# Scatters of different batches declared independent of each other, with a small memset ahead of each

## The chip, the cores and the metric

The kernel runs on one core of a Trainium2 chip. The metric is the device time of one execution in microseconds (us), the median of several runs. The core has five engines that run their own instruction streams side by side: TensorE (PE, matrix products), VectorE (DVE), ScalarE (ACT), GpSimd (POOL) and the sync engine (SP), which here issues plain transfers. They are tied together by semaphores. A transfer between the chip's main memory and the engines' memory is done by 16 DMA engines; an instruction only issues it, and a semaphore tells when it has landed.

## The reference

An attention with a sliding window feeds a layer in which only some tokens pass through an MLP (mixture of depths). There are 8 batches of 576 tokens, 8 heads of 64.

```python
# attention, window 128, with a linear bias by head
scores = scale * np.matmul(q, k.transpose(0, 1, 3, 2))
scores = np.where(mask, scores + bias[None], -1000000000.0)
attn = softmax(scores)                       # cut: written out in the reference
x = (attn @ v).transpose(0, 2, 1, 3).reshape(B, S, H * D)    # 8 x 576 x 512

# mixture of depths
scores = np.einsum('bsd,d->bs', x, w_gate)
out = x.copy()
for b in range(B):
    top_idx = np.argpartition(-scores[b], capacity)[:capacity]   # 128 of 576 tokens
    xe = x[b, top_idx]
    h = np.maximum(xe @ w1, 0.0)
    ye = h @ w2
    g = 1.0 / (1.0 + np.exp(-scores[b, top_idx]))
    out[b, top_idx] = x[b, top_idx] + g[:, None] * ye
```

For each batch, all 576 rows of `x` go to the output, and 128 of them get something added.

## The kernel before

The kernel is scheduled by hand: a list of words, `ORDER`, gives the order in which steps are issued, and each engine runs its own steps in that order. `b` is the batch. The output is built in two moves: `store` writes all rows of `x` of a batch (issued by the sync engine), and `scatter` adds the 128 changed rows with an indirect DMA that takes row numbers from `tok` (issued by GpSimd). The framework places waits between instructions that touch the same tensor. All stores and scatters touch the tensor `out`, so without further word each would wait for those before it; `declare_no_dep` tells the framework that a pair needs no wait.

```python
def store(b, part):
    if part == 0:
        i = SP.dma_start(out=out[b, 0:512, :]..., in_=x32[b][:, 0:4, :])      # cut
    else:
        i = SP.dma_start(out=out[b, 512:, :], in_=x32[b][:64, 4, :])
    stores.append((b, i))
    for o, j in scatters:
        tc.declare_no_dep(_ins(i), _ins(j), reason="other rows")

def w2(b):                                   # last product of a batch (TensorE), L654
    t = mm_t[b, "y"] = mx()
    for f in range(NFC):
        PE.matmul(out=t, lhsT=hs[b][:, f, :], rhs=w2_bf[:, f, :],
                  start=(f == 0), stop=(f == NFC - 1))

def w2_copy(b, eng):                         # its result times the gate: the rows to add, L661
    fin[b] = mod.tile([128, HD], fp32, name="fin", bufs=NFIN)        # NFIN = 4 buffers
    t = mm_t.pop((b, "y"))
    if eng is ACT:
        ACT.activation(out=fin[b], in_=t, func=AF.Identity, scale=gsel[b][:, 2:3])
    ...                                      # cut

def scatter(b):                              # L667
    i = POOL.indirect_dma_start(
        out=out.flatten_outer_dims(),
        out_offset=bass.IndirectOffsetOnAxis(ap=tok[b][:, :1], axis=0),
        in_=fin[b], in_offset=None, compute_op=OP.add)

    for o, j in stores:
        if o != b:
            tc.declare_no_dep(_ins(i), _ins(j), reason="other rows")
    scatters.append((b, i))
```

Before the change a scatter is thus free of the stores of other batches, but it waits for the stores of its own batch, for its rows, and for the scatter issued before it.

In `ORDER`, `Fb` is the scatter of batch b, `zb/A` is `w2_copy` on ScalarE, `Zb` is `w2`, `Wb0` and `Wb1` are the two halves of the first MLP product and `wb0`, `wb1` the copies of their results, `Ob` is the one-hot matrix `oh` that selects the tokens, `Db` the gather with it. The tail of the list (all of it is at the end of the whole kernel):

```text
J7 r6 H7
B7 h7/D O6/D Z5 b7/A E7 e6 M73 M70 D6 z5/A M72 F5 K6 M71 v6/A
k6 R7 e7 W61 F4 M74 r7 O7/D W60 w61/A D7 w60/A Z6 v7/D W71
z6/A F6 W70 w71/D K7 w70/A k7 Z7 z7/A F7
```

So the scatters are issued in the order of batches 0, 1, 2, 3, 5, 4, 6, 7, and the last instruction of the whole list is the scatter of batch 7.

Of the kernel before, what the change touches and what calls it, by code (L numbers as in the profile page):

```python
# [10 lines left out]
fp32 = mybir.dt.float32  # L11
# [15 lines left out]
def kernel(  # L27
# [12 lines left out]
    PE, DVE, ACT, POOL, SP = (nc.tensor, nc.vector, nc.scalar, nc.gpsimd,  # L40
                              nc.sync)
# [19 lines left out]
    const = ctx.enter_context(tc.tile_pool(name="const", bufs=1))  # L61
# [183 lines left out]
    def c_slope(c):  # L245
        def eo_(x):
            return x.rearrange("p (y s) -> p s y", s=2)
# [2 lines left out]
            in0=eo_(tmp[:, 1, :]), scalar=float(2.0 ** (2 - c)),  # L250
            in1=eo_(tmp[:, 0, :]), op0=OP.mult, op1=OP.add)

    ones_bf = const.tile([128, 128], bf16)
    neg1 = const.tile([128, 1], bf16)
    one_f = const.tile([128, 1], fp32)
# [214 lines left out]
    stores, scatters = [], []  # L470

    def _ins(i):
        return getattr(i, "inst", None) or getattr(i, "ins", i)
# [190 lines left out]
            DVE.tensor_scalar_mul(out=fin[b], in0=t, scalar1=gsel[b][:, 2:3])  # L664

    def scatter(b):
        i = POOL.indirect_dma_start(  # L667
            out=out.flatten_outer_dims(),
            out_offset=bass.IndirectOffsetOnAxis(ap=tok[b][:, :1], axis=0),
            in_=fin[b], in_offset=None, compute_op=OP.add)  # L670

        for o, j in stores:
            if o != b:
                tc.declare_no_dep(_ins(i), _ins(j), reason="other rows")
        scatters.append((b, i))

    wst = {}
# [215 lines left out]
```

## Time and profile before

| | before |
|---|---|
| time, median of 3 runs | 170.21 us (170.15 to 170.29) |
| span of the profiled execution | 168.3 us |
| TensorE busy | 129.8 us (77%) |
| VectorE busy | 127.8 us (76%) |
| ScalarE busy | 123.9 us (74%) |
| GpSimd busy | 105.4 us (63%) |
| scatters: GpSimd busy with them | 13.3 us, 8 of them, 1667 ns each in the mean |
| scatters: GpSimd idle ahead of them | 21.9 us |
| scatters: from start to landing, least / median / most | 4.6 / 4.7 / 7.0 us |

How to read it: the time is measured from outside, the span is that of one execution taken by the hardware profiler, a little shorter. A busy share is an average over the span; an engine that is busy three quarters of it can still set the end, and one that is rarely busy can be the one that all wait for at the end. For a scatter the profile shows two things: the time in which GpSimd writes the transfer's descriptors (`DMA_INDIRECT` on POOL, line 667), and the landing, known from its semaphore. In brackets behind an instruction stands the idle time of its engine just before it and what ended it; "issue" there means that the profile shows nothing that it waited for at that moment, often because another instruction of the queue held the wait.

Rows of the engines over the span are given in 40 equal slices, with a digit for the busy share in tenths.

### The profile page before, as it was taken

How to read it: one execution, taken by the hardware profiler on the slowest of the kernel's cores; microseconds unless marked ns; L12 is line 12 of the kernel's file. 1: busy time of each engine (PE TensorE's matmuls, PEld its weight loads, DVE VectorE, ACT ScalarE, POOL GpSimd, SP SyncE). 2: the span in 40 equal slices, each digit the busy share in tenths (PEclk: the TensorE clock that was granted, in tenths of full speed). 3: DMA queues.
4: the chain of work that ended last, by engine and by line, in shares of the span. 5: the costliest groups of instructions: out<-in, count | busy, mean ns of one | idle time of the engine just before them, and what ended most of it. 6: DMA issues, size and time to landing. Idle time of an engine off the chain costs nothing. (4 is left out here: it accounts for less than half of the span.)

```text
span 168.3 us, 5059 instructions
## 1 busy us (share of the span) xinstructions
PE 129.8 (77%) x2029; PEld 103.9 (62%) x2029; DVE 127.8 (76%) x378; ACT 123.9 (74%) x148; POOL 105.4 (63%) x168
## 2 busy tenths in 40 slices
PE   0165987778759869996599998999999999998200
PEld 0152766556649747995386987878588867686000
DVE  6885377989897899899868999898997898942000
ACT  1667679999888999969968997998987854423100
POOL 3835766659845996788299995785697813213330
PEclk9999999999978999999879999999999999999965
DMA  4999999999999999999999999999009349344224
GB/s 154 279 282 378 372 331 275 353 405 284 395 333 410 358 357 418 382 333 372 325 308 406 381 350 292 360 372 254 11 0 292 60 62 294 55 62 66 23 39 62
DMA packets 35216, 44.38 MB, mean 264 GB/s; under 512 B 1652, under 2 KB 24440, under 8 KB 35192
## 3 DMA queue, kind: packets, MB, share of 16 engines
q1 hardware_dynamic: 33464, 41.69, 75.2%
q0 software_dynamic: 1152, 2.10, 9.4%
q8 instruction: 16, 0.26, 0.6%
q10 hardware_dynamic: 576, 0.26, 0.6%
q14 instruction: 8, 0.07, 0.1%
HBM read 32.51 MB, written 11.53 MB: 262 GB/s over the span
## 5 line engine op out<-in xcount | busy, mean ns | idle before, releaser
L439 ACT ACTIVATE P<-sc 128x2048 bf16<-128x2048 f32 x32 | 60.1, 1877 | 9.6 <-PE sc L430 7.3
L307 POOL TENSOR_SCALAR_AFFINE_SELECT v_bf<-v_st 64x512 bf16<-64x512 f32 x42 | 30.7, 734 | 12.1 <-DMA v_st<-in_v_dram 10.3
L506 DVE CUSTOM_DVE_ANT_0 x_bf<-x,wg_bc 128x512 bf16<-128x512 f32 x35 | 28.1, 837 | 0.1
L466 DVE TENSOR_TENSOR x<-at,rc 128x640 f32<-128x640 f32 x32 | 26.4, 824 | 1.3 <-DVE rc L464 0.2
L667 POOL DMA_INDIRECT out_dram<-fin,tok x8 | 13.3, 1667 | 21.9 <-issue 11.8
L414 PE MATMUL sc<-mQ,mK 64*128 64x512 bf16 x128 | 20.8, 404 | 7.8 <-ACT P L439 7.8
L430 PEld LDWEIGHTS <-kT 64*128 64x128 bf16 x384 | 20.9, 114 | 8.7 <-issue 2.1
L457 PE MATMUL at<-v_bf,P 128*128 128x66 bf16 x320 | 24.3, 198 | 1.8 <-ACT P L439 0.9
L307 POOL TENSOR_SCALAR_AFFINE_SELECT q_bf<-q_st 128x576 bf16<-128x576 f32 x24 | 18.2, 779 | 9.1 <-DMA q_st<-in_q_dram 8.1
L457 PEld LDWEIGHTS <-P 128*128 128x128 bf16 x320 | 21.3, 101 | 2.3 <-ACT P L439 1.1
L454 PE MATMUL at<-v_bf,P 128*128 128x66 bf16 x256 | 22.1, 198 | 0.0
L430 PE MATMUL sc<-qT,kT 64*128 64x256 bf16 (+2 forms) x384 | 21.6, 248 | 0.0
L331 PE MATMUL mx<-ident_bf,q_bf 128*128 128x128 bf16 x144 | 13.4, 233 | 10.3 <-DVE q_bf L313 6.9
L547 DVE TENSOR_SCALAR_CACHE_REDUCE cmp<-row,sc_all 128x64 bf16<-128x64 f32 (+4 forms) x40 | 20.2, 537 | 0.8 <-ACT row L337 0.8
L454 PEld LDWEIGHTS <-P 128*128 128x128 bf16 x256 | 18.8, 101 | 0.7 <-issue 0.5
L307 POOL TENSOR_SCALAR_AFFINE_SELECT k_bf<-k_st 128x512 bf16<-128x512 f32 (+1 forms) x26 | 17.9, 704 | 0.5
L331 PEld LDWEIGHTS <-q_bf 128*128 128x128 bf16 x144 | 9.9, 104 | 11.9 <-DVE q_bf L313 6.9
L637 PE MATMUL mx<-gx,w_bf 128*128 128x128 bf16 x256 | 16.7, 219 | 0.4 <-DVE e_sb L609 0.3
L637 PEld LDWEIGHTS <-w_bf 128*128 128x128 bf16 x256 | 14.9, 98 | 1.4 <-ACT w_bf L695 0.3
L654 PE MATMUL mx<-w_bf,hs 128*128 128x512 bf16 x64 | 15.1, 379 | 0.6 <-ACT hs L647 0.6
L331 PE MATMUL mx<-ident_bf,k_bf 128*128 128x128 bf16 x144 | 13.1, 232 | 2.8 <-ACT hs L647 1.3
L337 ACT COPY qT<-mx 128x768 bf16<-128x768 bf16 (+1 forms) x17 | 13.1, 773 | 1.7 <-PE mx L331 1.6
(103 smaller groups left out, 224.5 us busy)
## 6 DMA issues: line engine op xcount, KB each, us to landing
v_st<-in_v_dram SPq DMA_DIRECT2D x16, 512.0 KB, 9.1
out_dram<-x SPq DMA_DIRECT2D x8, 1024.0 KB, 6.6
q_st<-in_q_dram SPq DMA_DIRECT2D x7, 1152.0 KB, 9.8
k_st<-in_k_dram SPq DMA_DIRECT2D x14, 512.0 KB, 9.1
x<-in_moe_w_dram SPq DMA_DIRECT2D x8, 512.0 KB, 8.4
k_st<-in_k_dram SPq DMA_DIRECT2D x4, 256.0 KB, 4.5
q_st<-in_q_dram SPq DMA_DIRECT2D x4, 256.0 KB, 3.8
v_tl<-in_v_dram SPq DMA_DIRECT2D x8, 128.0 KB, 6.8
```

What stands on the lines that cost most here:

```text
L307: POOL.affine_select(out=o, in_=i, compare_op=OP.is_ge, fill=0.0, base=1, pattern=[[0, n] for n in o.shape[1:]], channel_multiplier=0)
L331: PE.transpose(out=t[:, i, :], in_=qk_bf[b, w][:, r, :, :], identity=ident_bf)
L414: PE.matmul(out=sc[:, a, 512 * half:512 * half + 512], lhsT=mK[rows, c, :], rhs=(mQ[rows, :] if half else mQ[rows, None, 0:256].to_broadca ...
L430: PE.matmul(out=sc[:, a, c0:c0 + nq], lhsT=kc[rows, :], rhs=qt_[rows, S * c + q0:S * c + q0 + nq], start=False, stop=(c0 in (256, 832)))
L439: ACT.activation(out=p, in_=sc, func=AF.Exp, scale=scale)
L454: PE.matmul(out=o, lhsT=p[:, a, l:l + 128], rhs=vb[:, t - 1, h, :], start=True, stop=False)
L457: PE.matmul(out=o, lhsT=p[:, a, l:l + 128], rhs=vb[:, t, h, :], start=(t == 0), stop=True)
L466: DVE.tensor_tensor(out=xo[:, :, :, c, :], in0=av_[:, :, :, 0:D], in1=rc[:, :, :, None].to_broadcast([128, 2, NT, D]), op=OP.mult)
L506: DVE.tensor_tensor_reduce(out=part(x_bf[b][:, t, :]), in0=part(x32[b][:, t, :]), in1=part(wg_bc), scale=1.0, scalar=0.0, op0=OP.mult, op1 ...
L547: DVE.tensor_scalar(out=cmp_[b][:, t, 128 * t:], in0=row[b][:, 128 * t:], scalar1=sc_all[b][:, t:t + 1], scalar2=None, op0=OP.is_gt, op1=O ...
L637: PE.matmul(out=t[:, f, :], lhsT=w1_bf[:, dc, 128 * fg:128 * (fg + 1)], rhs=gx[b][:, dc, :], start=(dc == 0), stop=(dc == NDC - 1))
L654: PE.matmul(out=t, lhsT=hs[b][:, f, :], rhs=w2_bf[:, f, :], start=(f == 0), stop=(f == NFC - 1))
```

## The change

Scatters of different batches add to different rows of the output: batch b owns rows 576b to 576b+575. The change tells the framework so, for each pair of scatters, and the wait of a scatter for the one before it goes away. What is meant by it is that GpSimd can issue one scatter while another is still under way. Besides, a memset of a small tile of its own, `gap`, is put on GpSimd ahead of each scatter.

```diff
+    gap = const.tile([128, 1], fp32)
     ones_bf = const.tile([128, 128], bf16)
...
     def scatter(b):
+
+        POOL.memset(gap, 0.0)
         i = POOL.indirect_dma_start(
             out=out.flatten_outer_dims(),
             out_offset=bass.IndirectOffsetOnAxis(ap=tok[b][:, :1], axis=0),
@@
         for o, j in stores:
             if o != b:
                 tc.declare_no_dep(_ins(i), _ins(j), reason="other rows")
+        for _, j in scatters:
+            tc.declare_no_dep(_ins(i), _ins(j), reason="other rows")
         scatters.append((b, i))
```

In GpSimd's instruction stream of the changed kernel the scatters of batches 2, 3, 5, 4, 6 and 7 have lost one wait each, on the semaphore of the scatter before; all other waits for data and for stores are as they were.

## The prediction

> **What bounds the kernel now.** I read first where the engines stop working. The page's engine rows in 40 slices of 4.2 us:
>
> ```profile
> PE   0165987778759869996599998999999999998200
> DVE  6885377989897899899868999898997898942000
> ACT  1667679999888999969968997998987854423100
> POOL 3835766659845996788299995785697813213330
> ```
>
> TensorE, VectorE and ScalarE are dense up to slice 36 or so and empty in the last two or three; only GpSimd has work there. The last 10 us are a tail that belongs to GpSimd. The chain of work that ended last says the same:
>
> ```profile
> 156.85 1.54 DMA out_dram<-fin,tok
> 158.40 3.15 issue
> 161.54 0.04 POOLq L667
> 161.59 0.49 issue
> 162.07 1.76 POOLq L888
> ```
>
> From 156.85 us on it is one scatter (1.54 us of descriptor work, then 3.15 us until a semaphore wait of line 667 ends at 161.54), and then the next scatter. Between the two nothing computes: the later one waits for the earlier one to land. The third view is GpSimd's order in time from 125 us on:
>
> ```profile
> 126.05 1.83 POOL L667 DMA_INDIRECT out_dram<-fin,tok  x1 [0.16 <-POOL v_bf L307]
> ...
> 133.27 1.59 POOL L667 DMA_INDIRECT out_dram<-fin,tok  x1 [0.52 <-DMA out_dram<-fin,tok]
> 138.56 1.77 POOL L667 DMA_INDIRECT out_dram<-fin,tok  x1 [3.70 <-issue]
> 146.39 1.54 POOL L667 DMA_INDIRECT out_dram<-fin,tok  x1 [6.05 <-ACT fin L661]
> 151.31 1.54 POOL L667 DMA_INDIRECT out_dram<-fin,tok  x1 [3.38 <-DMA out_dram<-fin,tok]
> 156.85 1.54 POOL L667 DMA_INDIRECT out_dram<-fin,tok  x1 [4.00 <-issue]
> 162.30 1.54 POOL L667 DMA_INDIRECT out_dram<-fin,tok  x1 [3.90 <-issue]
> ```
>
> By the program these are the scatters of batches 1, 2, 3, 5, 4, 6, 7. Only batch 5's was released by its data (ACT fin). The last three follow each other at 4.92, 5.54 and 5.45 us, a serial chain. Against this I set ScalarE's order in time, where L661 writes the rows to be scattered:
>
> ```profile
> 145.41 0.69 ACT L661 ACTIVATE fin<-mx,e_sb 128x512 f32<-128x512 f32 x1 [1.03 <-PE mx L654]
> ...
> 152.16 0.69 ACT L661 ACTIVATE fin<-mx,e_sb 128x512 f32<-128x512 f32 x1 [2.26 <-PE mx L654]
> ...
> 156.64 0.69 ACT L661 ACTIVATE fin<-mx,e_sb 128x512 f32<-128x512 f32 x1 [1.99 <-PE mx L654]
> ```
>
> These are batches 5, 6 and 7. Batch 7's rows are ready at 156.64 + 0.69 = 157.33 us, but its scatter starts at 162.30: 4.97 us late. That is the whole prize, less what it costs to start.
>
> **What the Trainium skill says.** "DMA: Bandwidth & Descriptors", section "Anatomy of one DMA — SWDGE (gpsimd) path", puts a fixed cost of about 2.0 us on a DMA issued from GpSimd, mostly the receipt of the last write, plus its bytes over 436 GB/s. For 128 rows of 512 float32 (262 KB) my estimate from that page is 2.0 + 0.6 = 2.6 us. The trace shows 4.6 us from start to landing at best, of which 1.54 are GpSimd's own work, so 3.1 us after it: the same size, a little more (this one adds, so it reads the destination too). Most of it is latency, which a second scatter can share. The same page, section "Two DMAs through the same engine are not ordered", says that only a completion semaphore orders two DMAs. Scatters of different batches write disjoint rows (batch b owns rows 576b to 576b+575), so no order is needed among them. "SBUF — State Buffer", section "SBUF: two separate sides", warns that VectorE can lock GpSimd out while it writes descriptors. The trace fits mildly: 1.98 us for batch 0 and 1.83 for batch 1, beside a dense VectorE, 1.54 in the tail. And the first page again, section "SWDGE vs HWDGE vs iDMA", says that only one context is allocated to these DMAs. Whether that keeps one scatter from being written while another drains no trace here shows; it is a rival below.
>
> **The change, part by part.** Compared with the instruction streams of before, TensorE, VectorE, ScalarE and the sync engine have the same instructions with the same waits in the same order. GpSimd gets:
>
> *Added:* eight memsets of 128x1, one ahead of each scatter. A 128x1 memset takes 96 ns here (the rows of lines 279 and 281). Eight are 0.8 us of GpSimd, but each can run while GpSimd would be waiting for rows. In the tail: batch 7's memset follows batch 6's descriptors, near 154.7 us, 2.6 us before it could matter. On the path: 0.
>
> *Removed:* the wait for the previous scatter's landing, in six scatters (2, 3, 5, 4, 6, 7). All waits for data and for the same batch's own stores stay; the last stores (batch 7) are issued at 138.16 and 138.57 us, and take 6.6 us in the median (12.0 at most) to land, so they are done by about 151.
>
> *New start of each scatter.* From rows ready to start I take batch 5: 145.41 + 0.69 = 146.10, start at 146.39, so 0.29 us.
> - Batch 2: at most 0.5 us earlier, about 132.9 (GpSimd is busy with `oh` until 132.75).
> - Batch 3: its rows are ready at 136.38 + 0.69 = 137.07, so 137.36 instead of 138.56.
> - Batch 5: unchanged, 146.39.
> - Batch 4: its rows are long ready (140.75); right after batch 5's 1.54 us and a memset, about 148.2 instead of 151.31.
> - Batch 6: 152.16 + 0.69 + 0.29 = 153.14 instead of 156.85. GpSimd is free from about 149.8.
> - Batch 7: 157.33 + 0.29 = 157.62 instead of 162.30. GpSimd is free from about 154.8.
>
> *The end.* From batch 7's start to the end of the span it is 168.3 - 162.30 = 6.0 us now: 4.6 to landing at 166.9, where the sync engine's last semaphore waits begin, and 1.4 of closing. Batch 6 would land near 153.14 + 4.65 = 157.8, as batch 7 begins its descriptors, so the two transfers don't share time and I keep the 6.0. The gain is 162.30 - 157.62 = 4.68 us. Sum: 170.21 - 4.68 = 165.5 us; I write 165.6, with 0.1 us for small collisions of batch 4's scatter (below).
>
> What the chain of dependencies leading to batch 7's rows does stays as it is: its `fin` buffer is the one that batch 3 frees, at 138.56 + 7.0 = 145.6 at the latest now and earlier afterwards, and ScalarE waits for TensorE there (1.99 us), not for the buffer.
>
> **The rivals.**
> 1. *Descriptors of a second scatter can't be written until the first has drained* (one ring, one context). Then batch 4 starts at about 151.1, lands at 155.7, batch 6 starts at 155.8 and lands at 160.4, batch 7 starts at 160.5: gain 1.8 us, 168.4 us, within 2%. For it: no trace here has two in flight. Against it: after batch 0's scatter (113.34, 1.98 us) GpSimd's next cast starts at 114.79, so the engine is given back before the landing (5.5 us).
> 2. *Batch 4's descriptors collide with VectorE's one-hot of batch 7* (147.99, 0.82 us), which leads to batch 7's rows. If VectorE were stretched, the end would move with it. Another `oh` beside a GpSimd cast took 1.26 us instead of 0.82 (119.34), so up to 0.44 us: 166.0 us. Against it: VectorE's gate products beside batch 3's descriptors (138.33 to 140.33) take 0.56 us each, exactly as after it; there GpSimd was stretched to 1.77.
> 3. *Overlapping scatters land later.* Batches 1 and 3 took 7.0 us to land rather than 4.6 beside other transfers. If batch 7 met batch 6's end and landed 1 us later: 166.5. Against it: the descriptors of batches 6 and 7 come 4.5 us apart, and its transfer share is small (queue 0 used 9.4% of 16 engines' span for eight scatters: 0.094 x 168.3 / 8 = 2.0 us each).
> 4. *It's hidden anyway.* Then the gaps of 3.4 to 4.0 us would have ended at the data. They don't: batch 7's rows are 4.97 us early.
>
> **Range and chances.** The gain rests on durations measured in the same tail, and the runs of before lie within 0.14 us. I take 165.6 us; rivals 2 and 3 widen it upward, a quicker start by some tenths downward: 165.1 to 166.5. The 2% mark is at 166.81 us, so 1.2 us of the 4.7 may be lost before it is missed; only rival 1 loses as much. Faster by over 2%: 0.91; within: 0.07; slower by over 2%: 0.02, for something in the program of GpSimd that I don't see.
>
> **What would show it.** Right: on GpSimd's order in time the last two scatters start at about 153.1 and 157.6, both released by ACT fin of L661; batch 4 about 1.8 us behind batch 5; the last wait of the sync engine at about 162.3; span about 163.7. Wrong: a scatter that still starts some 4.6 us behind the one before (rival 1), a descriptor time well over 1.54 us in the tail, `oh` at 148 us over 0.82 us (rival 2), or a landing of batch 7 over 4.7 us (rival 3).

## The result and the profile after

| | before | changed |
|---|---|---|
| time, median of 4 runs each | 170.23 us (170.15 to 170.29) | 165.15 us (164.14 to 165.59) |
| ratio | | 0.9693, 95% interval 0.9645 to 0.9742 |
| span of the profiled execution | 168.3 us | 163.9 us |
| scatters: GpSimd idle ahead of them | 21.9 us | 16.6 us |

The change makes the kernel 3.1% faster, by 2.6 to 3.6%. The forecast was 165.6 us with a range from 165.1 up. The median lies at that edge; 0.9693 times 170.21, which rests on the means, is 165.0, just under it. The experiments below ask where those tenths are from. The profile of the changed kernel is that of its slowest execution, 165.59 us.

The same view as before, GpSimd in order of time, of the changed kernel from batch 3's scatter on (start, duration, engine and line, operation; in brackets the idle time just before and what ended it):

```profile
137.37 1.58 POOL L670 DMA_INDIRECT out_dram<-fin,tok  x1 [2.83 <-DVE rc L465]
138.35 0.71 POOL L669 MEMSET gap<- 128x1 f32 x1
146.39 1.55 POOL L670 DMA_INDIRECT out_dram<-fin,tok  x1 [7.33 <-ACT fin L662]
147.37 0.69 POOL L669 MEMSET gap<- 128x1 f32 x1
148.25 1.81 POOL L670 DMA_INDIRECT out_dram<-fin,tok  x1 [0.19 <-issue]
149.48 0.69 POOL L669 MEMSET gap<- 128x1 f32 x1
153.14 1.55 POOL L670 DMA_INDIRECT out_dram<-fin,tok  x1 [2.97 <-ACT fin L662]
154.11 0.70 POOL L669 MEMSET gap<- 128x1 f32 x1
157.62 1.55 POOL L670 DMA_INDIRECT out_dram<-fin,tok  x1 [2.81 <-ACT fin L662]
```

Batches 5, 6 and 7 are now each released by `ACT fin`, the copy that makes their rows. Batch 4 follows batch 5 after 1.86 us, with batch 5's transfer still under way. The last two scatters start at 153.14 and 157.62 us, to the hundredth the figures in the prediction. Part of that is luck: batch 5's scatter happens to start at 146.39 us in both profiles, and other executions differ there by more than a microsecond (below). ScalarE's rows of batch 7, in its order of time:

```profile
156.66 0.69 ACT L662 ACTIVATE fin<-mx,e_sb 128x512 f32<-128x512 f32 x1 [1.99 <-PE mx L655]
```

They were written from 156.64 us on in the kernel before: in these two executions computing runs alike, and the whole difference is that the scatter no longer stands in a queue behind others. From start to landing a scatter takes (least, median, most) in the kernel before

```profile
DMA to landing us min/median/max: 4.6/4.7/7.0
```

and in the changed one

```profile
DMA to landing us min/median/max: 4.8/5.1/7.5
```

A little longer now. From batch 7's start to the end it is 163.9 - 157.62 = 6.3 us instead of 6.0 (spans are given to a tenth): 4.8 us instead of 4.6 to its landing, and 1.4 us of closing in both. And the chain that ended last, by engine, which in the kernel before consisted of the last scatters alone, now goes back through the computing:

```profile
PE 44%; DMA 30%; DVE 11%; ACT 4%; issue 3%; POOL 3%; SPq 1%; POOLq 1%; ACTq 0%
```

### The profile page after: what moved, and what is told of

Its sections match the earlier page's. It is cut to its first block, busy times and chain, and to the rows that moved or that the text cites. A ratio compares the mean times of both kernels' runs of the same rounds, so it can differ in the third digit from the quotient of the medians.

```text
span 163.9 us, 5063 instructions
## 1 busy us (share of the span) xinstructions
PE 130.8 (80%) x2029; PEld 104.3 (64%) x2029; DVE 127.9 (78%) x378; ACT 124.3 (76%) x148; POOL 104.0 (63%) x176
## 4 chain that ended last, share of the span: by engine, by line
PE 44%; DMA 30%; DVE 11%; ACT 4%; issue 3%; POOL 3%; SPq 1%; POOLq 1%; ACTq 0%
DMA q_st<-in_q_dram 12%; PE mx L655 7%; PE mx L638 7%; DMA k_st<-in_k_dram 6%; DMA x<-in_moe_w_dram 6%; PE sc L415 6%; PE sc L431 5%; DMA v_tl<-in_v_dram 5%; DVE x_bf L507 5%; PE mx L624 4%; PE mx L332 4%; PE at L458 3%; ACT P L440 2%; POOL q_bf L308 2%; PE at L455 2%
## 5 line engine op out<-in xcount | busy, mean ns | idle before, releaser
L308 POOL TENSOR_SCALAR_AFFINE_SELECT v_bf<-v_st 64x512 bf16<-64x512 f32 x42 | 29.8, 712 | 12.8 <-DMA v_st<-in_v_dram 8.0
L507 DVE CUSTOM_DVE_ANT_0 x_bf<-x,wg_bc 128x512 bf16<-128x512 f32 x35 | 28.7, 855 | 0.4 <-PE mx L624 0.3
L670 POOL DMA_INDIRECT out_dram<-fin,tok x8 | 13.0, 1622 | 16.6 <-ACT fin L662 13.1
L308 POOL TENSOR_SCALAR_AFFINE_SELECT k_bf<-k_st 128x512 bf16<-128x512 f32 (+1 forms) x26 | 17.3, 681 | 1.0 <-DMA k_st<-in_k_dram 0.6
L332 PE MATMUL mx<-ident_bf,k_bf 128*128 128x128 bf16 x144 | 13.6, 237 | 2.9 <-DVE kT L340 1.1
L340 DVE COPY kT<-mx 128x1024 bf16<-128x1024 bf16 (+1 forms) x23 | 11.8, 527 | 3.7 <-PE mx L332 3.5
```

Of the source, the lines that this page charges most:

```text
L308: POOL.affine_select(out=o, in_=i, compare_op=OP.is_ge, fill=0.0, base=1, pattern=[[0, n] for n in o.shape[1:]], channel_multiplier=0)
L332: PE.transpose(out=t[:, i, :], in_=qk_bf[b, w][:, r, :, :], identity=ident_bf)
L507: DVE.tensor_tensor_reduce(out=part(x_bf[b][:, t, :]), in0=part(x32[b][:, t, :]), in1=part(wg_bc), scale=1.0, scalar=0.0, op0=OP.mult, op1 ...
```

## The experiments

**First theory: the kernel before is held, the changed one is free.** Before, the four first runs lay within 0.14 us; changed, they spread over 1.45 us. My theory was that the chain of landings, of nearly fixed length, holds the kernel before from batch 1 on, while the changed kernel ends when its computing ends, and so moves with TensorE's granted clock (a share of full speed; 1 is full). Its rivals: the transfers vary, or the chips and sessions do. The next four kernels ran on one chip.

*The changed kernel again.*

> The changed kernel once more, for its spread. My theory: its end is now the end of the computing (batch 7's rows ready) plus a constant tail of 6.5 us, so it moves with the clock that TensorE is granted; the kernel before is held by a serial chain of scatter landings from batch 1 on and does not. Then single times between 164.0 and 165.7 us, spread over 1 us or more, shorter at a higher clock, with the kernel before within 0.3 us of 170.2 in the same rounds; and in the profile the start of batch 7's scatter moves by what the span moves, span minus that start staying at 6.2 to 6.3 us. Rival (the transfers vary: overlapping scatters drain in more or less time): batch 7's scatter starts at 157.6 us in every profile, and the tail after it varies by the microsecond. Rival (chips or sessions differ): the kernel before varies as much.

Measured: 0.9736 (0.9686 to 0.9787), median 165.29 us, single runs 164.5 to 165.9 us. But the kernel before did not lie within 0.3 us: 24 runs of it went from 168.9 to 171.2 us (three more, over 1.5% above the fastest, are left out, as such executions are in all ratios and ranges here). Nor does the mean granted clock sort them: 169.04 us came at 0.951, 170.76 at 0.970. Of the five runs of the changed kernel, 164.48 us came at 0.967 and 164.99 at 0.990. The small spread before, the ground of the theory, was an accident of four runs. One part of it held: in the profile batch 7's scatter starts at 156.51 us, 1.11 us earlier than in the first profile, and the span is 162.7, 1.2 us shorter; what is saved is saved before that scatter, not behind it.

```profile
145.28 1.55 POOL L670 DMA_INDIRECT out_dram<-fin,tok  x1 [7.33 <-ACT fin L662]
...
156.51 1.55 POOL L670 DMA_INDIRECT out_dram<-fin,tok  x1 [2.81 <-ACT fin L662]
```

From batch 5's scatter to batch 7's it is 11.23 us here and 11.23 us in the first profile.

*The memsets alone.*

```diff
+        POOL.memset(gap, 0.0)          # kept
-        for _, j in scatters:          # left out
-            tc.declare_no_dep(_ins(i), _ins(j), reason="other rows")
```

> The eight memsets alone, all waits between scatters kept. Both theories: 170.2 us, within 0.3, spread like the kernel before. If the memsets themselves shift anything (order of waits, landing), it shows here as a difference of more than 0.3 us.

Measured: 1.0013 (0.9990 to 1.0037). The memsets cost nothing that can be seen, so the gain comes from the waits taken away. Whether it would be as large without the memsets was not run.

*Only the last scatter freed.*

```diff
-        for _, j in scatters:
+        for _, j in (scatters if b == 7 else []):
```

> Only the scatter of batch 7 is freed of the scatter before it; batches 1, 2, 3, 5, 4, 6 keep their serial chain. Batch 6 starts at 156.85 us as in the kernel before, batch 7 after its descriptors and a memset at about 158.6, and lands 5.3 us later if two that start 1.8 us apart drain one behind the other (as batches 5 and 4 do in the changed kernel), 4.7 us later if they don't hinder each other: 167.1 or 166.5 us. Theory of the held chain: the times are as steady as those of the kernel before, within 0.4 us, since batch 6 is still chained. Rival (spread comes from overlapping transfers): a spread of 1 us or more, since two scatters overlap right at the end.

Measured: 0.9837 (0.9779 to 0.9895), single runs 166.4 to 168.6 us. With batch 6 still in the chain, the spread is as wide as anywhere, against the first theory. The tail of its profile:

```profile
151.89 1.55 POOL L670 DMA_INDIRECT out_dram<-fin,tok  x1 [3.37 <-DMA out_dram<-fin,tok]
...
157.51 1.55 POOL L670 DMA_INDIRECT out_dram<-fin,tok  x1 [3.96 <-issue]
158.49 0.69 POOL L669 MEMSET gap<- 128x1 f32 x1
159.37 1.55 POOL L670 DMA_INDIRECT out_dram<-fin,tok  x1 [0.19 <-issue]
```

Batch 7 starts 1.86 us behind batch 6 instead of 5.45. It lands 5.2 us after its start, at 164.6, and batch 6 lands 4.6 us after its own, at 162.2; so the landings are 2.4 us apart, the starts 1.86. That fits transfers that drain one behind the other (5.3 us was expected then, 4.7 otherwise); the times alone don't separate the two.

*All freed but the last.*

```diff
-        for _, j in scatters:
+        for _, j in (scatters if b < 7 else []):
```

> All scatters freed but that of batch 7, which waits for the others, batch 6 last, to land. Batch 6 starts with its rows at 153.14 us, lands at 157.9, batch 7 starts 0.75 us later at about 158.7 instead of 157.6: 1.0 us slower than the changed kernel, 166.2 us in the median. Theory of the held chain: the spread is that of the changed kernel (1 us or more), because batch 6 follows the computing. Rival (spread comes from overlapping at the end): steady within 0.4 us, since the last two don't overlap.

Measured: 0.9817 (0.9772 to 0.9862), single runs 166.1 to 167.1 us. Batch 7's scatter starts 12.49 us behind batch 5's, 1.26 more than in the changed kernel:

```profile
153.46 1.55 POOL L670 DMA_INDIRECT out_dram<-fin,tok  x1 [2.98 <-ACT fin L662]
154.44 0.69 POOL L669 MEMSET gap<- 128x1 f32 x1
159.20 1.55 POOL L670 DMA_INDIRECT out_dram<-fin,tok  x1 [4.07 <-DMA out_dram<-fin,tok]
```

I had expected 1.0 us. Batch 6 lands 4.8 us after its start, and from there to the next start it takes 0.95 us, where the kernel before took 0.83 and I had put 0.75. Three semaphore instructions of this scatter stand in between, at 158.3 to 158.4 us, where the kernel before has one for its last scatter. Freeing the last scatter alone gives 1.6%, freeing all the others 1.8%, and both 2.6 to 3.1%: either way the tail shrinks only to what the remaining link leaves.

**Second theory: the gain is the tail from batch 5's scatter on, and the rest is chance from before it.** Two questions are left. Does the chain begin with batch 5's rows, or do earlier landings hold the kernel before as well? And does the end of the changed kernel follow batch 7's rows? Two edits, each made in both kernels.

*Batch 7's last product in another order.* The first four of its eight matmuls use the half of `hs` that is ready earlier; the result is copied half on ScalarE, half on VectorE.

```diff
-            W70 w71/D K7 w70/A k7 Z7 z7/A F7
+            W70 w71/D Z70 w70/A K7 k7 Z71 z7/A F7     # Z70: f = 4..7, Z71: f = 0..3
+        if b == B - 1:                                # in w2_copy
+            ACT.activation(out=fin[b][:, 0:256], in_=t[:, 0:256], ...)
+            DVE.tensor_scalar_mul(out=fin[b][:, 256:512], in0=t[:, 256:512], ...)
+            return
```

> The kernel before with the last product of batch 7 taken in another order: its first four matmuls use the half of hs that is ready earlier and run while the other half is still being copied, and its result is copied half on ScalarE, half on VectorE. Batch 7's rows should be ready 0.9 to 1.1 us earlier. Theory (the end of the kernel before is the chain of landings from batch 5 on): no change, within 0.3 us of the kernel before in the same rounds; in the profile batch 7's scatter still follows batch 6's by 5.4 to 5.6 us. Rival (computing still sets a part of the end): up to 1.0 us faster.

> The same edit on the changed kernel. Theory (its end is batch 7's rows plus 0.3 us to start and a tail of about 6.2 us): 0.9 to 1.1 us faster than the changed kernel, 164.2 to 164.4 us in the median; batch 7's scatter starts 10.2 to 10.4 us behind batch 5's in the profile instead of 11.2, span minus its start stays 6.2. Rival (GpSimd or the transfers bound the tail now): the start moves but the landing doesn't, 165.2 us.

Measured: before with this edit 0.9986 (0.9959 to 1.0012), changed with it 0.9705 (0.9665 to 0.9746). In time neither kernel shows a clear gain (the changed one stands at 0.9711 without the edit, the mean of its three ratios in this document), so the profiles have to tell. In the kernel before batch 7's rows are ready 10.50 us behind batch 5's scatter instead of 10.94, and nothing comes of it; its last scatters still stand 5.27 and 5.51 us apart:

```profile
146.30 1.54 POOL L677 DMA_INDIRECT out_dram<-fin,tok  x1 [5.07 <-ACT fin L671]
151.12 1.54 POOL L677 DMA_INDIRECT out_dram<-fin,tok  x1 [3.28 <-DMA out_dram<-fin,tok]
156.39 1.54 POOL L677 DMA_INDIRECT out_dram<-fin,tok  x1 [3.73 <-ACT fin L665]
161.90 1.54 POOL L677 DMA_INDIRECT out_dram<-fin,tok  x1 [3.97 <-issue]
```

In the third line `ACT fin` is ScalarE's half of batch 7's copy, which ended at 156.29, by chance near the start of batch 6's scatter; that one does not need it.

In the changed kernel the distance from batch 5 to batch 7 falls from 11.23 to 10.78 us, half of what I expected. The two half copies in the trace:

```profile
155.71 0.47 ACT L666 ACTIVATE fin<-mx,e_sb 128x256 f32<-128x256 f32 x1 [1.24 <-PE mx L659]
156.22 0.48 DVE L668 TENSOR_SCALAR fin<-mx,e_sb 128x256 f32<-128x256 f32 x1 [1.04 <-ACT fin L666]
156.98 1.55 POOL L680 DMA_INDIRECT out_dram<-fin,tok  x1 [2.36 <-DVE fin L668]
```

VectorE's half waits for ScalarE's (the program has that wait), so 0.47 and 0.48 us stand one after the other in the place of 0.69. The splitting took back 0.3 us of what the order gave.

*Less computing for batch 7.* The sixteen matmuls that put bias and mask on the scores of batch 7 are left out, so its output is that of another computation.

```diff
-        for half in (0, 1):
+        for half in ((0, 1) if b < B - 1 else ()):
...
-                          start=False, stop=(c0 in (256, 832)))
+                          start=(b == B - 1),
+                          stop=(b == B - 1 or c0 in (256, 832)))
```

> The kernel before without the sixteen matmuls that put bias and mask on the scores of batch 7 (left out; its output for batch 7 is then that of another computation). They take 0.6 us for each of four head pairs between 121 and 133 us, so computing for batches 5, 4, 6 and 7 can run 1.0 to 2.4 us earlier from there. Theory (serial landings hold the kernel before already from batch 1 on, with batch 5's rows just in time: batch 3 lands at 145.6, batch 5 starts at 146.4): 0.0 to 0.4 us faster, and batch 5's scatter is then released by a landing and not by ScalarE. Rival (the chain begins with batch 5's rows): as much faster as the changed kernel with the same edit, 1.0 to 2.4 us.

> The same left out of the changed kernel. Both: no scatter waits for another, so the whole of the time saved in computing reaches the end: 1.0 to 2.4 us faster than the changed kernel, 162.9 to 164.3 us; batches 5, 6 and 7 released by ScalarE, 11.2 us from batch 5's scatter to batch 7's.

Measured: before with less computing 0.9948 (0.9923 to 0.9973), changed with less 0.9666 (0.9623 to 0.9709). The kernel before gains 0.5%, 0.9 us; the changed one, against 0.9711, 0.45%, 0.8 us, with an uncertainty nearly as large. Less was saved than I had thought, but no less in the kernel before. The profile of the kernel before with less computing decides against my theory that landings hold it from batch 1 on, and for the rival, that the chain begins with batch 5's rows (GpSimd's two scatters, then ScalarE's copy of batch 5's rows):

```profile
137.52 1.74 POOL L668 DMA_INDIRECT out_dram<-fin,tok  x1 [3.80 <-ACT gx L337]
144.81 1.54 POOL L668 DMA_INDIRECT out_dram<-fin,tok  x1 [5.55 <-ACT fin L662]
```

```profile
143.85 0.69 ACT L662 ACTIVATE fin<-mx,e_sb 128x512 f32<-128x512 f32 x1 [1.03 <-PE mx L655]
```

Batch 3's scatter, the first line, lands 6.4 us later at 143.9; batch 5's starts only at 144.81, 0.27 us behind its rows (143.85 + 0.69 = 144.54). The margin is small: rows ready more than some 0.6 us earlier would have met that landing.

**Where the spread is from.** Nothing of the change runs before the first scatter at 113 us; up to there all kernels have the same instructions but for one memset. The starts of three instructions in each profile and its span, in us (the 19th of 32 exponentials of the attention lies in the middle of the kernel):

| kernel | 19th exponential (ScalarE) | batch 5's scatter | batch 7's scatter | span |
|---|---|---|---|---|
| before | 85.57 | 146.39 | 162.30 | 168.3 |
| memsets alone | 85.12 | 145.96 | 162.09 | 168.2 |
| before, other order | 84.72 | 146.30 | 161.90 | 167.9 |
| last freed | 86.09 | 146.86 | 159.37 | 166.0 |
| all but last freed | 85.38 | 146.71 | 159.20 | 165.4 |
| changed | 85.15 | 146.39 | 157.62 | 163.9 |
| changed, again | 84.42 | 145.28 | 156.51 | 162.7 |
| changed, third time | 84.96 | 146.09 | 157.75 | 163.9 |
| changed, other order | 85.04 | 146.20 | 156.98 | 163.1 |

The same work reaches the 19th exponential anywhere from 84.42 to 86.09 us, and batch 5's scatter from 145.28 to 146.86. From batch 5 to batch 7 it is 15.60 to 16.13 us with the chain whole and 11.23 to 11.66 us with it gone and the order unchanged. So 1.6 us of spread arises in front of the tail, in kernels of both kinds. What moves there, I did not find out. TensorE's granted clock is a candidate: ahead of the tail the traces show it at half for stretches of 3.4 us. There are two of these in most of the profiles and three in the two with the latest batch 5 (146.71 and 146.86). But the first profile of the changed kernel has four at 146.39, and with two alone the start goes from 145.28 to 146.39, so they are not the whole of it. Longer times come with a lower mean clock in the ten runs of the kernel before beside the third measurement of the changed one (correlation -0.66), but hardly in the 24 above (-0.24).

**A faster kernel, and a third interval.** The order of the last product was altered without the split copy, on the changed kernel, twice; and the changed kernel ran once more beside the first of them.

```diff
-        if b == B - 1:                 # the split copy of above taken out again
-            ...
```

> The changed kernel with only the order of batch 7's last product altered (the four matmuls on the earlier half of hs first); its result is copied by ScalarE alone, as before, since the half on VectorE waited for the half on ScalarE (0.47 and 0.48 us one after the other, instead of 0.69). Theory (the end is batch 7's rows plus a constant): batch 7's scatter starts 10.5 us behind batch 5's, 0.7 us less than in the changed kernel and 0.3 less than with the split copy; 0.7 us faster than the changed kernel in the same rounds. Rival (another bound is near): 10.8 us as with the split copy, or no gain in the time.

> The changed kernel a third time, beside the one above. If the gain is only the tail from batch 5's scatter on (4.7 us less 0.2), the ratio to the kernel before is 0.9735 give or take what the part before 112 us does by chance: between 0.970 and 0.976. If the first measurement (0.9693) was right and something outside the tail gains 0.4 us more, 0.969 or less again.

> The changed kernel with the altered order of batch 7's last product once more, for a second interval and a profile. Theory (the end is batch 7's rows plus a constant): batch 7's scatter starts 10.5 us behind batch 5's, span minus its start 6.2 us, ratio to the kernel before 0.966 to 0.970, which is 0.7 us below the changed kernel. Rival (no more gain than the first product order left by chance): 0.971 or more, or a distance of 11.2 us.

Measured: 0.9667 (0.9626 to 0.9707) and 0.9673 (0.9628 to 0.9717) with the other order; 0.9705 (0.9658 to 0.9751) for the changed kernel. The two agree at 0.967, the three of the changed kernel have a mean of 0.9711, so the other order brings 0.4%, 0.7 us, as expected, though single intervals overlap and don't prove it. In the two profiles batch 7's scatter starts 10.47 and 10.93 us behind batch 5's, where 10.5 was expected; they are of the longest execution of each run (167.07 and 166.9 us), so nothing is rested on them. This is the fastest version of the study: about 164.6 us where the kernel before takes 170.2. In the third profile of the changed kernel, batch 7's scatter came 11.66 us behind batch 5's. The 0.43 us more lie between TensorE's last one-hot product and ScalarE's copy of `hs`, both ends without a visible cause:

```profile
154.20 0.60 ACT L648 ACTIVATE hs<-mx 128x512 bf16<-128x512 f32 x1 [1.64 <-PE mx L604]
```

In the second profile of it that idle time was 1.20 us. It stays open.

## Why the prediction was right and where it was off

- *What bounds:* right. The last three scatters were a chain, and batch 7's rows lay ready 4.97 us; with them ready 0.4 us earlier the last scatters still stood 5.27 and 5.51 us apart.
- *New starts:* right to 0.05 us for batches 5, 4, 6 and 7 (148.25 against 148.2), batch 3 at 137.37 against 137.36, batch 2 at 132.83 against 132.9. The delays from rows to start are right; that the absolute times agree is chance, because batch 5 started at 146.39 us in both profiles.
- *Memsets cost nothing on the path:* right, 1.0013.
- *The 6.0 us from batch 7's start to the end:* 6.3 in the first profile, 6.1 to 6.2 in later ones, so the term was some 0.1 to 0.2 us short. The memsets alone, with all waits kept, had 6.1 too.
- *"Most of it is latency, which a second scatter can share":* wrong. The prediction's estimate puts 0.6 us on moving the rows; in the trace, which decides, a lone scatter's packets fill 2.2 to 2.4 of the 3.1 us behind the descriptor work. It cost nothing here, because batch 7 comes 4.5 us behind batch 6: in the first profile batch 6's packets end at 157.6 us and batch 7's begin at 159.8.
- *Rival 1, a scatter's descriptors wait for the one before to drain:* refuted. They were written 1.86 us apart.
- *Rival 2, batch 4's descriptors stretch VectorE's one-hot:* refuted; `oh` took 0.83 us beside them (0.82 before). GpSimd was stretched instead, 1.81 us for 1.54. So the 0.1 us put on top for collisions was not needed. The line of `oh` in the changed kernel, to be set beside batch 4's scatter at 148.25:

```profile
147.80 0.83 DVE L594 TENSOR_TENSOR oh<-krow,rank 128x640 bf16<-128x640 f32 x1
```

- *Rival 3, overlapping scatters land later:* true for batch 4, 5.3 us. Batch 7, whose neighbour is 4.5 us away, took 4.8, a tenth over the 4.7 given as the sign of it; in the other two profiles of the changed kernel it took 4.7, as with the memsets alone, so that this tenth comes from the overlap is not shown.
- *The step that failed* is the start of the sum, "Batch 5: unchanged, 146.39", with its ground in "Range and chances", "the runs of before lie within 0.14 us". The cost of everything ahead of the tail was taken as the same in every execution, and the lower edge set 0.5 us under the point. In its place the profiles show batch 5's scatter starting anywhere from 145.28 to 146.86 us, in kernels of both kinds. 24 runs of the kernel before in a later session lie between 168.9 and 171.2 us, and the four of the changed kernel between 164.1 and 165.6. The profiled one of these four, with batch 5 at 146.39, took 165.59 us, which is the point forecast; the shorter three have no profile. The second profile has batch 5 1.11 us earlier, the same 11.23 us behind it, and a span 1.2 us shorter. So that the missing tenths lie ahead of the tail is the likely reading, and what moves there stays open. The range should have reached at least 0.8 us to each side, half of the spread of batch 5's start.

The predicted gain itself, 4.68 us less 0.2 for the longer landing, is a ratio of 0.974; the three measured are 0.9693, 0.9736 and 0.9705, and all three intervals hold it, the first one barely. That something outside the tail gains another 0.4 us is not excluded: their mean is 4.9 us. The profiles show no place for it; from batch 5 to the end the kinds differ by 15.9 + 6.1 against 11.4 + 6.2 us, 4.4 us.

## What to carry to other kernels

Where independent transfers stand in a chain only because they write one tensor, compare the time each one's data is ready with the time it starts: the last one's delay, less what it costs to start, is the gain, and after it the end follows the computing, so that small edits there begin to count. Declare the independence for every link of the tail; freeing only the last link, or all but the last, left some two fifths of the gain behind (1.6 and 1.8% of 2.9). And take a kernel's spread from many runs, not from three that agree.

## What was not expected of the hardware

- GpSimd takes up its next instruction before a scatter's descriptors are done: as the trace records it, the memset begins 0.98 us into a scatter's 1.55 us and takes 0.69 us, where a lone one took 0.10. The next scatter could start 1.86 us behind the first.
- Two scatters close together drain one behind the other. In the first profile of the changed kernel the packets of batches 5 and 4 filled 4.7 us without a pause; a lone scatter's fill 2.2 to 2.4 us. What overlaps is descriptor work and the way to landing, not the transfer: over the profiles the second lands 5.0 to 5.4 us after its start, where a lone one in the tail took 4.4 to 4.9.
- Beside VectorE's one-hot, which reads two operands from the engines' memory, it is the descriptor work that stretches (1.81, in one execution 2.04 us), not VectorE (0.83 us in each). The transfer in flight is not the reason: with only the last scatter freed, batch 7's descriptors were written 1.86 us behind batch 6's, with VectorE at rest, in 1.55 us.
